# Store issue, layer norm steps and weight splitting rearranged in a kernel of spectral and sliding-window layers

## The chip, the cores and the metric

The kernel runs on one core of one Trainium2 chip. The time is the device time of one execution in microseconds (us); three executions of the kernel before gave 2269.78, 2270.76 and 2272.49 us, median 2270.76 us. One profiled execution gives the trace from which everything below is read.

## The reference

Four layers work on x of 2048 rows (S) and 640 columns (D), all in float32: a spectral (FNet) layer, a sliding-window attention block, and both again with the same weights. Each adds to x a function of the layer norm of x.

```python
# spectral: real part of a DFT over the columns, then over the rows
a = einsum("bsd,ed->bse", x, dft_hid_re);  b = einsum("bsd,ed->bse", x, dft_hid_im)
y = einsum("ts,bse->bte", dft_seq_re, a) - einsum("ts,bse->bte", dft_seq_im, b)
# attention: 32 heads of 20, each row sees itself and the 255 rows before it
q, k, v = split(x @ wqkv);  p = softmax(mask(q k^T * 20**-0.5));  out = (p v) @ wo
# layer norm, without weights: (x - mean) / sqrt(var + 1e-5)
```

## The kernel before, in words

Every float32 operand of TensorE is kept as two float16 parts, hi and lo; a product of two operands takes three float16 matmuls (hi·hi, hi·lo, lo·hi) that add up in PSUM. In almost every split ScalarE writes hi (an ACTIVATE that casts), and VectorE or GpSimd writes lo (the value less hi).

**The spectral layer.** x is 16 tiles of 128 rows. For each tile a `z_stage` makes the DFT over the columns (tiles `zc`). Then come four passes r over groups of 4 tiles of x, and in each pass eight steps j, each for two output tiles. A step (r, j) multiplies with seven combinations of blocks of the row DFT matrix, so that 7 products stand in place of 8: 7 products of 12 matmuls (128 columns by 320). The matrix blocks come as one 1 MB load `cq` per step (`load_c`, L170 through the helper `load`), two steps ahead. `take_c` makes the seven combinations of the next step: GpSimd forms four sums `cs` (L473 to L476), ScalarE writes each hi part `cc` (L481) and VectorE each lo part (L484). The products leave PSUM by one ACTIVATE (L520) and six VectorE adds (L507) per step, and GpSimd adds three more pieces (L521, L531, L542). The sums gather in two `res` tiles per step; there are 4 buffers. In passes 1 to 3 `res` is first loaded from `acc_d`; at the end of a step (`main_c`, L556) it is stored to `acc_d`, in the last pass to `x2_d`.

**What runs beside it.** `tick()` is called after each product (7 times a step). It issues one waiting split of `cc` and moves each generator of the list `side` to its next `yield`. So the number of `yield`s in a generator sets how it is spread over the products. In the first spectral layer the side generators are: `side_norm` (layer norm of one tile of x for the next pass, 12 in all, at j = 3, 4, 6, 7), `keep_w` (stores of the split column DFT matrix), `b_max` (largest values of the attention weights, 20 reductions), then `b_scale` and `b_split`, which scales, splits and stores the attention weights in 15 chunks of 128 by 640: ScalarE writes scaled hi (L653), VectorE scaled lo (L655, tile `bst`), ScalarE's queue stores both (L658). In pass 3 of both spectral layers `finish` normalizes the first tiles of the result for the attention (two tiles at a time), and `ahead` makes the first q and k products (`qk`) from them. `fill_stack` loads the first `ks` tiles of the attention at j = 7.

**Layer norm.** `norm_steps` takes n = 1 or 2 tiles at once: mean and variance on VectorE (L127, L130), then the inverse root in a column of n values: four TENSOR_SCALARs (L134 to L137: add epsilon, a shift and a subtraction on the bits for a first guess, a scaled copy), then three Newton steps (L141 and L145 for n = 1; L143, L144 and L145 for n = 2), tile `lnt`. The last step, (x − mean)·g over 128 by 640, is VectorE's L149, tile `lny`. `split` then writes `xs` (ScalarE L161, GpSimd L162). There are 30 calls with n = 1 and 17 with n = 2: 2 and 1 at the start, 12 in `side_norm`, 4 (n = 2) in `finish`, and 16 and 12 in the attention blocks. That makes 64 tiles.

**What sets the order.** Each engine runs its instructions in the order in which they were issued to its queue, and a DMA issue that has to wait holds up what is behind it on the engine that issues it. All loads go through `load`, on SyncE (SP). The 160 stores of this change (128 of `res`, 30 of `bst`, 2 of the column DFT matrix) are on ScalarE's queue; the stores of the q and k products (`qkd`) are on SP already.

Of the kernel before, what the change touches and what calls it, by code (L numbers as in the profile page):

```python
# [13 lines left out]
I32 = mybir.dt.int32  # L14
# [31 lines left out]
BACK_LAG = 15  # L46
M_UP = 2.0 ** 15
# [4 lines left out]
X_UP = 2.0 ** 10  # L52
# [8 lines left out]
def body(ctx: ExitStack, tc: tile.TileContext, x_in, cmat, whid, wqkv, wo, out):  # L61
# [58 lines left out]
    def norm_steps(xs, ys):  # L120

        n = len(xs)
        mv = keep.tile([P, n, 2], F32, tag=f"lnmv{n}", name="lnmv", bufs=2)
        for k, x in enumerate(xs):
            st = keep.tile([P, 2, 6], F32, tag="lnst", name="lnst", bufs=2)
            for h in range(2):
                nc.vector.bn_stats(st[:, h], x[:, h * 320:(h + 1) * 320])  # L127
                if h == 0:
                    yield
            nc.vector.bn_aggr(mv[:, k], st.rearrange("p a b -> p (a b)"))  # L130
            yield
        t = keep.tile([P, 3, n], F32, tag=f"lnt{n}", name="lnt", bufs=2)
        v, g, u = t[:, 0], t[:, 1], t[:, 2]
        nc.vector.tensor_scalar(v, mv[:, :, 1], 1e-5, X_UP ** -2, op0=OP.add, op1=OP.mult)  # L134
        nc.vector.tensor_scalar(g.bitcast(I32), v.bitcast(I32), 1, None, op0=OP.logical_shift_right)
        nc.vector.tensor_scalar(v, v, -0.5, None, op0=OP.mult)
        nc.vector.tensor_scalar(g.bitcast(I32), g.bitcast(I32), -1, 0x5F3759DF, op0=OP.mult, op1=OP.add)  # L137
        yield
        for k in range(3):
            if n == 1:  # L140
                nc.vector.scalar_tensor_tensor(u, g, v, g, op0=OP.mult, op1=OP.mult)  # L141
            else:
                nc.vector.tensor_tensor(u, g, g, op=OP.mult)  # L143
                nc.vector.tensor_tensor(u, u, v, op=OP.mult)  # L144
            nc.vector.scalar_tensor_tensor(g, u, 1.5, g, op0=OP.add, op1=OP.mult)  # L145
            yield
        for k, x in enumerate(xs):
            y = keep.tile([P, D], F32, tag="lny", name="lny", bufs=2)
            normed[0] = nc.vector.tensor_scalar(y, x, mv[:, k, 0:1], g[:, k:k + 1],  # L149
                                                op0=OP.subtract, op1=OP.mult).ins  # L150
            ys.append(y)
            yield
# [187 lines left out]
    def spectral(layer, res_src, hidden, first):  # L340
        with ExitStack() as st:
# [95 lines left out]
            def side_norm(s):  # L437
                x, ys = load_x(s), []
                for _ in range(3):
                    yield 1  # L440
                for _ in norm_steps([x], ys):
                    yield 1
                split_x(s, ys[0], nc.gpsimd)
                yield 1
# [101 lines left out]
            def main_c(r, j):  # L546
# [8 lines left out]
                for k in range(2):  # L555
                    nc.scalar.dma_start((x2_d if last else acc_d)[2 * j + k], res[k])  # L556
# [16 lines left out]
            def finish(j, pace):  # L573
# [6 lines left out]
                for _ in norm_steps(xs, ys):  # L580
                    for _ in range(pace):
                        yield 1
                for y in ys:
                    xs = keep.tile([P, 2, D], F16, tag="xs", name="xs", bufs=2)
                    split(xs[:, 0], xs[:, 1], y, nc.gpsimd)
                    xss.append(xs)
                    yield 1
# [18 lines left out]
            def b_max():  # L606
# [3 lines left out]
                for n in range(20):  # L610
# [3 lines left out]
                    for _ in range(2):  # L614
                        yield 1
# [29 lines left out]
            def b_split(n0, n1):  # L645
# [3 lines left out]
                for n in range(n0, n1):  # L649
# [3 lines left out]
                    nc.scalar.activation(hi, f, AF.Copy, scale=sc)  # L653
                    yield 1
                    nc.vector.scalar_tensor_tensor(lo, f, sc, hi, op0=OP.mult, op1=OP.subtract)  # L655
                    cs = slice((n % 3) * D, (n % 3 + 1) * D)
                    for k in range(2):
                        nc.scalar.dma_start(bw_d[k][:, n // 3, cs], t[:, k])  # L658
# [5 lines left out]
            def keep_w():  # L664
                for k in range(2):
                    nc.scalar.dma_start(w_d[k], w[:, k].rearrange("p a b c -> p (a b c)"))
# [20 lines left out]
            for r in range(NR):  # L687
# [22 lines left out]
                for j in range(NJ):  # L710
                    n = r * NJ + j
                    if first:
                        if (r, j) == (0, 1):
                            side.append(chain(keep_w(), b_max()))
                        if (r, j) == (1, 0):
# [584 lines left out]
```

## Time and profile before

| | |
|---|---|
| runs | 2269.78, 2270.76, 2272.49 us |
| the profiled execution | 2268.34 us, its span 2266.6 us |
| granted TensorE clock, mean of the span | 0.988 |
| PE (TensorE) busy | 2131.3 us, 94% |
| DVE (VectorE) busy | 1699.9 us, 75% |
| POOL (GpSimd) busy | 1364.0 us, 60% |
| ACT (ScalarE) busy | 1263.9 us, 56% |

Times in the trace are counted from the span's start. The first spectral layer takes about the first 600 us, the first attention block the next 550, the second spectral layer ends near 1700 us, the second attention block is the rest. A row of windows gives, for a stretch, its length and for PE, weight loads (PEld), DVE, ACT and POOL the busy us and, in brackets, the number of instructions; then the granted clock, the share of the DMA engines that was busy, and GB/s. A row of groups has line, engine, operation, out<-in, shape, count | busy us, mean ns of one | idle us of the engine just before them and what ended it. A row of waits has who waited <- for whom: us in all, times, longest. A row of the timeline has start, duration, engine, line, operation.

### The profile page before, as it was taken

To read this page: it belongs to the slowest core of one execution; us is meant where nothing else is said; L and a number is where in the kernel's file an instruction comes from. 1 tells how busy PE (TensorE), PEld (TensorE's weight loads), DVE (VectorE), ACT (ScalarE), POOL (GpSimd) and SP (SyncE) were. 2 spreads that over 40 slices of the span, in tenths; PEclk is the share of its full clock that TensorE was granted. 3 is DMA by queue.
4 is the path that set the end of the run, shared out by engine and by line. 5 is a ranking of instruction groups with operands and counts; after the bars stand their busy time and mean duration, and the time that the engine had idled before them with its cause. 6 is when DMAs were issued, how large, how long until landed. Compare 5 with 4: busy or idle time off the path is not lost.

```text
span 2266.6 us, 55134 instructions
## 1 busy us (share of the span) xinstructions
PE 2131.3 (94%) x21985; PEld 1498.0 (66%) x21985; DVE 1699.9 (75%) x3601; ACT 1263.9 (56%) x2120; POOL 1364.0 (60%) x1773
## 2 busy tenths in 40 slices
PE   7989899999899999999899999999898999999997
PEld 5667567667566676667556777777675666667765
DVE  7887969867678888887757858585776877777664
ACT  5334344343367777777754343434334777777775
POOL 5766758757355655566445858586683555556543
PEclk9999999999999999999999999999999999999999
DMA  5763656454432422332324536354643323332231
GB/s 190 281 223 124 230 161 208 145 198 163 134 77 69 107 70 69 95 90 75 133 73 149 197 122 207 119 201 146 236 140 97 83 61 86 79 90 68 55 81 36
DMA packets 187606, 292.95 MB, mean 129 GB/s; under 512 B 13908, under 2 KB 120660, under 8 KB 178004
## 3 DMA queue, kind: packets, MB, share of 16 engines
q1 hardware_dynamic: 163732, 238.63, 35.2%
q10 hardware_dynamic: 23616, 50.80, 6.1%
q8 instruction: 172, 2.82, 0.5%
q14 instruction: 86, 0.70, 0.1%
HBM read 202.51 MB, written 86.87 MB: 128 GB/s over the span
## 4 chain that ended last, share of the span: by engine, by line
PE 66%; DVE 21%; DMA 5%; issue 4%; ACT 2%; POOL 2%; SPq 0%; DVEq 0%; ACTq 0%; POOLq 0%
PE pf L114 26%; PE y L114 9%; PE pv L114 8%; PE z L114 6%; PE x L114 6%; PE sp L114 5%; DVE cc L484 5%; DVE m L1054 3%; PE tp L114 3%; DVE sp L1050 2%; PE pt L114 2%; DVE res L507 1%; DVE lnt L145 1%; DMA x2d<-res 1%; DVE lny L149 1%
## 5 line engine op out<-in xcount | busy, mean ns | idle before, releaser
L114 PEld LDWEIGHTS <-cc 128*128 128x128 f16 x5376 | 529.3, 99 | 245.8 <-issue 38.3
L1098 ACT ACTIVATE ptq<-tp,shift,alpha 128x768 f32<-128x768 f32 (+2 forms) x512 | 486.2, 950 | 161.7 <-PE tp L114 153.2
L114 PEld LDWEIGHTS <-big 128*128 128x128 f16 x4320 | 407.7, 98 | 136.4 <-issue 26.1
L1054 DVE TENSOR_REDUCE m<-sp 128x2 f32<-128x512 f32 (+1 forms) x512 | 345.1, 674 | 17.2
L1050 DVE COPY_PREDICATED sp<-mask,sp 128x256 f32<-128x256 int32 x448 | 190.6, 426 | 183.6 <-PE sp L114 168.3
L1103 POOL TENSOR_SCALAR_AFFINE_SELECT ptq<-ptq 128x512 f32<-128x512 f32 x224 | 145.9, 651 | 278.7 <-ACT ptq L1098 273.2
L114 PE MATMUL pf<-early,big 128*128 128x256 f16 x2400 | 313.3, 273 | 0.0
L481 ACT ACTIVATE cc<-cs 128x512 f16<-128x512 f32 x256 | 152.3, 623 | 249.4 <-POOL cs L474 100.6
L114 PE MATMUL y<-zc,cc 128*128 128x320 f16 x1728 | 270.9, 305 | 14.5 <-DVE pf L507 14.5
L114 PE MATMUL pf<-big 128*128 128x320 f16 x1680 | 242.2, 301 | 9.1 <-DVE early L252 4.2
L484 DVE SCALAR_TENSOR_TENSOR cc<-cs,cc 128x512 f16<-128x512 f32 x256 | 232.6, 924 | 3.6 <-ACT cc L481 3.6
L484 DVE SCALAR_TENSOR_TENSOR cc<-cq,cc 128x512 f16<-128x512 f32 x192 | 201.8, 1052 | 0.0
L1105 POOL TENSOR_SCALAR_AFFINE_SELECT ptq<-ptq 128x512 f32<-128x512 f32 x256 | 163.1, 637 | 42.5 <-ACT ptq L1098 42.5
L114 PE MATMUL z<-zc,cc 128*128 128x320 f16 x1152 | 179.7, 301 | 6.3 <-DVE res L507 6.3
L114 PE MATMUL pv<-ptq,v 128*32 128x128 f32 (+1 forms) x3840 | 183.8, 331 | 0.0
L114 PE MATMUL x<-zc,cc 128*128 128x320 f16 x1152 | 181.6, 301 | 0.0
L114 PE MATMUL sp<-ks,qs 62*128 62x256 f16 (+1 forms) x1792 | 153.3, 248 | 23.7 <-DVE m L1054 20.2
L114 PE MATMUL pf<-big,early 128*128 128x320 f16 x960 | 163.0, 300 | 8.1 <-DVE x L875 8.1
L114 PE MATMUL tp<-qs,ks 62*128 62x128 f16 x2688 | 150.1, 217 | 4.3 <-ACT ptq L1098 3.8
L1075 ACT ACTIVATE qs<-pt 2x512 f16<-2x512 f16 x224 | 130.9, 585 | 38.3 <-PE pt L114 36.3
L114 PE MATMUL pf<-bo,ot 128*128 128x320 f16 x840 | 144.1, 300 | 1.6 <-DVE ot L948 1.6
L114 PEld LDWEIGHTS <-ks 62*128 62x128 f16 x3008 | 116.1, 94 | 42.7 <-DVE m L1054 20.0
(144 smaller groups left out, 3526.8 us busy)
## 6 DMA issues: line engine op xcount, KB each, us to landing
cq<-in_cmat_dram SPq DMA_DIRECT2D x64, 1024.0 KB
accd<-res ACTq DMA_DIRECT2D x96, 320.0 KB
res<-accd SPq DMA_DIRECT2D x96, 320.0 KB
x<-x2d SPq DMA_DIRECT2D x64, 320.0 KB
qkd<-early SPq DMA_DIRECT2D x160, 128.0 KB
ks<-qkd SPq DMA_DIRECT2D x108, 160.0 KB
qs<-qkd SPq DMA_DIRECT2D x84, 160.0 KB
x2d<-res ACTq DMA_DIRECT2D x32, 320.0 KB
```

The source lines that it names most:

```text
L114: i = getattr(nc.tensor, what)(*args, **kw)
L145: nc.vector.scalar_tensor_tensor(g, u, 1.5, g, op0=OP.add, op1=OP.mult)
L149: normed[0] = nc.vector.tensor_scalar(y, x, mv[:, k, 0:1], g[:, k:k + 1], op0=OP.subtract, op1=OP.mult).ins
L481: nc.scalar.activation(cc[m][:, 0], f, AF.Copy, scale=C_UP)
L484: nc.vector.scalar_tensor_tensor(cc[m][:, 1], f, C_UP, cc[m][:, 0], op0=OP.mult, op1=OP.subtract)
L507: marks["dve"] = nc.vector.scalar_tensor_tensor(o, z, Y_DOWN, f, op0=OP.mult, op1=OP.add).ins
L1050: nc.vector.copy_predicated(sp[:, :, 2 * P:3 * P], mask[:, None, :].to_broadcast([P, 2, P]), far)
L1054: topped[0] = nc.vector.tensor_reduce(TOP[g // 4][:, g % 4], sp[:, :, c0:3 * P], axis=AX.X, op=OP.max).ins
L1075: nc.scalar.activation(o, handed[n][rs].rearrange("r (i p) t -> r i p t", i=2), AF.Copy)
L1098: nc.scalar.activation(q[:, h:h + 2, a0 + first:a0 + 3], tp[:, :, first * P:3 * P].rearrange("p a (b c) -> p a b c", c=P), AF.Sigmoid, bia ...
L1103: nc.gpsimd.affine_select(out=q[:, :, a0], in_=q[:, :, a0], pattern=[[0, 4], [-1, P]], base=0, channel_multiplier=1, compare_op=OP.is_gt, ...
L1105: ins = nc.gpsimd.affine_select(out=q[:, :, a0 + 2], in_=q[:, :, a0 + 2], pattern=[[0, 4], [1, P]], base=0, channel_multiplier=-1, compare ...
```

## The change

Four things:

1. The stores of `res`, of `bst` and of the column DFT matrix go through `load`, so on SP's queue, in order with the loads.
2. `norm_steps` works on one 128x1 column per tile. Every step is a TENSOR_SCALAR with one tensor input and up to two per-partition scalars; the first guess is one step (a multiplication by −0.5 and an addition on the bits as integers). A call with n = 1 has 8 such steps instead of 10, one with n = 2 has 16 instead of 13. `side_norm` and `finish` call it with `act=True`: then one more step per tile makes −mean·g, the last step over 128 by 640 is ScalarE's `activation(Identity, bias, scale)`, and two more `yield`s stand ahead of it. That moves 20 of the 64 `lny` from VectorE to ScalarE. All root steps together go from 521 to 532.
3. `b_split`: ScalarE scales the chunk in place and writes hi (two ACTIVATEs), GpSimd subtracts (L663), in place of one ACTIVATE and VectorE's L655.
4. Pacing: `b_scale` and `b_split` start at step (1, 2) instead of (1, 0); `b_max` has one more `yield` per chunk; `finish` has three more beside those of the norm, so that `qk` comes later.

Lines above L141 shift by up to 8: L170 is L175 in the changed kernel, L484 is L489, L507 is L512, L473 to L476 are L478 to L481.

```diff
-        v, g, u = t[:, 0], t[:, 1], t[:, 2]
-        nc.vector.tensor_scalar(v, mv[:, :, 1], 1e-5, X_UP ** -2, op0=OP.add, op1=OP.mult)
-        nc.vector.tensor_scalar(g.bitcast(I32), v.bitcast(I32), 1, None, op0=OP.logical_shift_right)
-        nc.vector.tensor_scalar(v, v, -0.5, None, op0=OP.mult)
-        nc.vector.tensor_scalar(g.bitcast(I32), g.bitcast(I32), -1, 0x5F3759DF, op0=OP.mult, op1=OP.add)
-        yield
-        for k in range(3):
-            if n == 1:
-                nc.vector.scalar_tensor_tensor(u, g, v, g, op0=OP.mult, op1=OP.mult)
-            else:
-                nc.vector.tensor_tensor(u, g, g, op=OP.mult)
-                nc.vector.tensor_tensor(u, u, v, op=OP.mult)
-            nc.vector.scalar_tensor_tensor(g, u, 1.5, g, op0=OP.add, op1=OP.mult)
+        ts = nc.vector.tensor_scalar
+        for k in range(n):
+            h, g, u = (t[:, m, k:k + 1] for m in range(3))
+            ts(h, mv[:, k, 1:2], 1e-5, -0.5 * X_UP ** -2, op0=OP.add, op1=OP.mult)
+            ts(g.bitcast(I32), h.bitcast(I32), -0.5, ROOT, op0=OP.mult, op1=OP.add)
+            for m in range(3):
+                ts(u, g, g, h, op0=OP.mult, op1=OP.mult)
+                normed[0] = ts(g, u, 1.5, g, op0=OP.add, op1=OP.mult).ins
+                if m == 0:
+                    yield
+            if act:
+                normed[0] = ts(u, mv[:, k, 0:1], g, -1.0, op0=OP.mult, op1=OP.mult).ins
+            yield
+        for _ in range(2 if act else 0):
             yield
         for k, x in enumerate(xs):
+            g, u = t[:, 1, k:k + 1], t[:, 2, k:k + 1]
             y = keep.tile([P, D], F32, tag="lny", name="lny", bufs=2)
-            normed[0] = nc.vector.tensor_scalar(y, x, mv[:, k, 0:1], g[:, k:k + 1],
-                                                op0=OP.subtract, op1=OP.mult).ins
+            if act:
+                nc.scalar.activation(y, x, AF.Identity, bias=u, scale=g)
+            else:
+                normed[0] = ts(y, x, mv[:, k, 0:1], g, op0=OP.subtract, op1=OP.mult).ins
...
                 for k in range(2):
-                    nc.scalar.dma_start((x2_d if last else acc_d)[2 * j + k], res[k])
+                    load((x2_d if last else acc_d)[2 * j + k], res[k])
...
+                    yield 1
+                for _ in range(2):
                     yield 1
                 proj.new_rows(j)
...
-                    nc.scalar.activation(hi, f, AF.Copy, scale=sc)
+                    nc.scalar.activation(f, f, AF.Copy, scale=sc)
+                    nc.scalar.activation(hi, f, AF.Copy)
                     yield 1
-                    nc.vector.scalar_tensor_tensor(lo, f, sc, hi, op0=OP.mult, op1=OP.subtract)
+                    nc.gpsimd.tensor_tensor(lo, f, hi, op=OP.subtract)
                     cs = slice((n % 3) * D, (n % 3 + 1) * D)
                     for k in range(2):
-                        nc.scalar.dma_start(bw_d[k][:, n // 3, cs], t[:, k])
+                        load(bw_d[k][:, n // 3, cs], t[:, k])
...
-                        if (r, j) == (1, 0):
+                        if (r, j) == (1, 2):
                             side.append(chain(b_scale(), b_split(0, 15)))
```

On VectorE, inside pass 1 or 2 of the first spectral layer, a side norm stands between the lo parts (`cc`) and the adds (`res`, `pf`). Before, with a chunk of `b_split` (`bst`) just ahead of it:

```order
L655 SCALAR_TENSOR_TENSOR bst<-wst,wsc,bst 128x640
L134 TENSOR_SCALAR lnt<-lnmv 128x1
L507 SCALAR_TENSOR_TENSOR res<-y,res 128x320
L135 TENSOR_SCALAR lnt<-lnt 128x1
L484 SCALAR_TENSOR_TENSOR cc<-cq,cc 128x512
L136 TENSOR_SCALAR lnt<-lnt 128x1
L137 TENSOR_SCALAR lnt<-lnt 128x1
L141 SCALAR_TENSOR_TENSOR lnt<-lnt 128x1
L145 SCALAR_TENSOR_TENSOR lnt<-lnt 128x1
L507 SCALAR_TENSOR_TENSOR pf<-y,pf 128x320
```

The same kind of place in the changed kernel, where line 140 and 141 are the two steps of a Newton round and L145 makes −mean·g:

```order
L489 SCALAR_TENSOR_TENSOR cc<-cs,cc 128x512
L137 TENSOR_SCALAR lnt<-lnmv 128x1
L138 TENSOR_SCALAR lnt<-lnt 128x1
L140 TENSOR_SCALAR lnt<-lnt 128x1
L141 TENSOR_SCALAR lnt<-lnt 128x1
L512 SCALAR_TENSOR_TENSOR pf<-y,pf 128x320
L489 SCALAR_TENSOR_TENSOR cc<-cs,cc 128x512
L140 TENSOR_SCALAR lnt<-lnt 128x1
L489 SCALAR_TENSOR_TENSOR cc<-cs,cc 128x512
L141 TENSOR_SCALAR lnt<-lnt 128x1
```

The two-input steps on `lnt` and the chunk of `bst` are gone from VectorE's queue; the lo parts and adds stay.

On GpSimd, in pass 1 of the first spectral layer, one step j of sums `cs` and adds to `res`. Before, with the split of a normed tile (`xs`) in it:

```order
L521 TENSOR_TENSOR res<-res,pf 128x320
L473 TENSOR_TENSOR cs<-cq 128x512
L475 TENSOR_TENSOR cs<-cq 128x512
L474 TENSOR_TENSOR cs<-cs,cq 128x512
L476 TENSOR_TENSOR cs<-cq,cs 128x512
L531 TENSOR_TENSOR res<-res,pf 128x320
```

Now:

```order
L526 TENSOR_TENSOR res<-res,pf 128x320
L478 TENSOR_TENSOR cs<-cq 128x512
L480 TENSOR_TENSOR cs<-cq 128x512
L479 TENSOR_TENSOR cs<-cs,cq 128x512
L663 TENSOR_TENSOR bst<-wst,bst 128x640
L481 TENSOR_TENSOR cs<-cq,cs 128x512
L536 TENSOR_TENSOR res<-res,pf 128x320
```

A chunk of the weights stands ahead of the fourth sum.

On SP, in the first spectral layer (the numbers tell the tiles apart: accd6 is the seventh tile of `acc_d`, `cq` the matrix blocks of a step, `wst` and `xin` chunks of the weights and of x). Before, only loads:

```order
L170 DMA res_2757<-accd6_117 128x640
L170 DMA res_2758<-accd7_118 128x640
L170 DMA cq_2748<-in_cmat_dram 128x2048
L170 DMA wst_2837<-in_wqkv_dram 128x640
L170 DMA res_2910<-accd8_119 128x640
L170 DMA res_2911<-accd9_120 128x640
```

Now the stores of `res` and `bst` stand between them, the loads of accd8 and accd9 and of `cq` behind the stores of accd4 and accd5:

```order
L175 DMA accd4_115<-res_2580 128x640
L175 DMA bwd0_145<-bst_2795 128x640
L175 DMA accd5_116<-res_2581 128x640
L175 DMA bwd1_146<-bst_2795 128x640
L175 DMA res_2895<-accd8_119 128x640
L175 DMA xin_2918<-in_x_dram 128x640
L175 DMA res_2896<-accd9_120 128x640
L175 DMA cq_2886<-in_cmat_dram 128x2048
```

More of the change, by code (lines that the diff above doesn't have):

```diff
@@ L46 @@
 BACK_LAG = 15
+ROOT = float(0x5F3759DF - (1 << 22) - (1 << 30))
 M_UP = 2.0 ** 15
@@ L118, in body, with norm_steps @@
     matmul, transpose = partial(tensor, "matmul"), partial(tensor, "transpose")
-    def norm_steps(xs, ys):
+    def norm_steps(xs, ys, act=False):
         n = len(xs)
@@ L440, in side_norm @@
                     yield 1
-                for _ in norm_steps([x], ys):
+                for _ in norm_steps([x], ys, True):
                     yield 1
@@ L579, in finish @@
                 ys, xss = [], []
-                for _ in norm_steps(xs, ys):
+                for _ in norm_steps(xs, ys, True):
                     for _ in range(pace):
@@ L613, in b_max @@
                         fs.append(b_chunk(n + 3))
-                    for _ in range(2):
+                    for _ in range(3):
                         yield 1
@@ L665, in keep_w @@
                 for k in range(2):
-                    nc.scalar.dma_start(w_d[k], w[:, k].rearrange("p a b c -> p (a b c)"))
+                    load(w_d[k], w[:, k].rearrange("p a b c -> p (a b c)"))
                     yield 1
```

## The prediction

> **What bounds the kernel now.** I read the page's chain first. TensorE carries two thirds of it, VectorE a fifth, and ScalarE, GpSimd and SP almost none:
>
> ```profile
> PE 66%; DVE 21%; DMA 5%; issue 4%; ACT 2%; POOL 2%; SPq 0%; DVEq 0%; ACTq 0%; POOLq 0%
> ```
>
> Then the windows. The two spectral layers do the same products, but only the first has side norms and weight splits beside them. So I set 500 us of the first beside 500 us of the second, then the 200 us in which the weights are split, then 50 us of the second layer:
>
> ```profile
> 100.00:600.00 500.00, 461.89 (x3391) 329.40 (x3389) 392.96 (x708) 196.39 (x383) 329.70 (x276) 0.97 0.55 183
> 1200.00:1700.00 500.00, 491.13 (x3642) 354.91 (x3641) 355.67 (x562) 197.02 (x398) 355.98 (x299) 0.99 0.51 170
> 250.00:450.00 200.00, 183.65 (x1329) 129.74 (x1329) 167.82 (x293) 86.31 (x164) 137.32 (x109) 0.97 0.55 183
> ...
> 1500.00:1550.00 50.00, 49.88 (x369) 35.81 (x367) 41.42 (x57) 19.46 (x37) 42.44 (x31) 1.00 0.61 207
> ```
>
> PE is idle 38.1 us in the first stretch and 8.9 in the second: 29.2 us more. The clock costs another 461.89 x 0.02/0.99 = 9.3. So the first layer runs 38 us behind the second. DVE is busy 393 us of the 500 there against 356. The longest waits of PE in the first stretch name DVE:
>
> ```profile
> PE y L114 <- DVE pf L507: 19.7, 9, 4.2
> PE pf L114 <- DVE early L252: 4.2, 2, 3.2
> ```
>
> L507 is the add that frees a PSUM bank; it comes late because other work stands ahead of it on DVE. The lower clock belongs to the stalls, as PE's timeline shows just behind one: these 12 matmuls take 3.15 us, the same 12 take 1.79 in the row after.
>
> ```profile
> 252.99 3.15 PE L114 MATMUL y<-zc,cc 128*128 128x320 f16 x12 [4.18 <-DVE pf L507]
> 255.98 1.79 PE L114 MATMUL x<-zc,cc 128*128 128x320 f16 x12
> ```
>
> **Root steps and lny.** Three windows of 100 to 600 us, each of one tile, give what the change touches on DVE: `lnt` (steps and lny together), `lny`, `bst`.
>
> ```profile
> 100.00:600.00 500.00, 62.71 (x162) 0.97 0.55 183
> ```
>
> ```profile
> 100.00:600.00 500.00, 16.48 (x16) 11.70 (x16) 25.30 (x16) 0.97 0.55 183
> ```
>
> ```profile
> 100.00:600.00 500.00, 20.82 (x15) 12.28 (x15) 0.97 0.55 183
> ```
>
> The steps alone are 62.7 - 16.5 = 46.2 us for 162 - 16 = 146 instructions (12 norms of n = 1 by 10, 2 of n = 2 by 13). The change makes them 12 x 9 + 2 x 18 = 144. Nothing is won by their number, so all hangs on the duration of one. The same window's groups, and the whole trace's figures for L141 (min/median/max):
>
> ```profile
> L141 DVE SCALAR_TENSOR_TENSOR lnt<-lnt 128x1 f32<-128x1 f32 x36 | 14.1, 391 | 0.5
> ...
> L135 DVE TENSOR_SCALAR lnt<-lnt 128x1 int32<-128x1 int32 x12 | 1.8, 148 | 0.2
> ```
>
> ```profile
> L141 DVE SCALAR_TENSOR_TENSOR lnt<-lnt x90: 203/214/1230, 6.8 to 1205.5; 128x1 f32<-128x1 f32 x90
> ```
>
> Two tensor inputs took 391 ns in the mean but 214 in the median; one input took 148. The timeline shows where the long ones come from:
>
> ```profile
> 382.34 1.60 POOL L476 TENSOR_TENSOR cs<-cq,cs 128x512 f32<-128x512 f32 x1
> ...
> 382.91 0.15 DVE L135 TENSOR_SCALAR lnt<-lnt 128x1 int32<-128x1 int32 x1
> ...
> 383.91 1.30 POOL L531 TENSOR_TENSOR res<-res,pf 128x320 f32<-128x320 f32 x1
> 384.42 0.81 DVE L141 SCALAR_TENSOR_TENSOR lnt<-lnt 128x1 f32<-128x1 f32 x1
> ```
>
> L141 ends about when GpSimd's L531 does, at 385.2; L135 ran its 0.15 us inside GpSimd's L476. So a two-input step waits for GpSimd and a one-input step does not. The new steps have one tensor input, but two per-partition scalars, which no step of the trace has in a 128x1 column. Bounds: 148 ns (one input) gives 144 x 0.148 = 21.3 us, a saving of 24.9; 391 ns (two inputs, with waits) gives 56.3, a loss of 10.1. I take L141's undisturbed 214, since the scalars have to be read: 30.8 us, saving 15.4. The rule that speaks against it stands in the Trainium skill, VectorE: DVE Perf Modes, "Rules for kernel authors": for chained operations, do not fuse for speed, minimize their number. By that rule 146 against 144 saves nothing; the rows of 148 and 391 ns at equal size say that number alone does not decide here.
>
> All 16 lny of the window leave DVE: 16.5 us. ScalarE takes them, at
>
> ```profile
> L161 ACT ACTIVATE xs<-lny 128x640 f16<-128x640 f32 x16 | 11.7, 731 | 23.5 <-DVE lny L149 23.5
> ```
>
> 0.73 us each for the same size: 12 us, and 15 more ACTIVATEs in b_split another 12, on an engine busy 196 of 500. Its cover is that idle time; if ACT's high parts came late by it, the price is in the next paragraph's halves.
>
> **b_split.** DVE loses all 15 L655: 20.8 us. GpSimd gains 15 subtractions of 128x640, priced by its nearest row of this window:
>
> ```profile
> L162 POOL TENSOR_TENSOR xs<-lny,xs 128x640 f16<-128x640 f32 x16 | 25.3, 1581 | 12.4 <-ACT xs L161 12.4
> ```
>
> 15 x 1.58 = 23.7 us. While they run, DVE's two-input lo parts can wait: from 0 to all of 23.7; I take half, 11.9. DVE thus goes down by 15.4 + 16.5 + 20.8 - 11.9 = 40.8, to 352 of 500, and GpSimd up to 353: the levels of the second layer (356 and 356), where PE loses 38 us less.
>
> I do not take all of it. The chunks come every 6 ticks; 6 products of 1.79 us are 10.7, so all 15 fall within 161 us, inside the 250:450 stretch. GpSimd there goes to (137.3 + 23.7)/200 = 80%. Excess of that stretch: 16.35 idle + 183.65 x 0.02/0.99 = 3.7, less 8.87 x 0.4 = 3.5 as in the second layer: 16.5. I take half back, 8, and of the other 22 all but 3, since b_max's reductions stay on DVE: 19. Together **27 us**, bounds 0 to 38.
>
> **Stores on SP.** 160 issues leave ACT. The waits of ACT in the window and of SP in the whole trace:
>
> ```profile
> ACT cc L481 <- DVE res L507: 20.0, 11, 3.9
> ```
>
> ```profile
> SPq L170 <- DMA accd<-res: 316.9, 84, 12.5
> ...
> SPq L170 <- DVE bst L655: 49.9, 12, 17.7
> ```
>
> ACT's high part stood behind a store that waited for `res`: 20 us go, off the path (ACT has room; 2% of the chain). SP already waits for these very stores to land before it reloads the same four buffers, 3.8 us on the mean, and for `bst`, up to 17.7 us; `cq` comes two steps ahead. So I price the move at nothing; the cover is that step in hand, and the price without it is a rival.
>
> **Layer ends and attention.** At the end of the second spectral layer (1640 to 1730 us) PE waits for DVE's adds:
>
> ```profile
> PE z L114 <- DVE res L507: 2.3, 1, 2.3
> ...
> PE y L114 <- DVE pf L507: 0.6, 1, 0.6
> PE sp L114 <- DVE res L507: 0.6, 1, 0.6
> ```
>
> 3.5 us per layer. In each layer's `finish` 4 lny leave DVE and 26 steps become 36 shorter ones. I take 2 of the 3.5 back per layer: **4 us**. Bounds: 8 and -5, the latter if the `qk` products, 4 products (7 us) later by their yields, leave the first attention rows late by 2.5 us per layer.
>
> In the attention blocks lny stays; `lnt` and then `lny` in the two blocks:
>
> ```profile
> 600.00:1200.00 600.00, 82.90 (x257) 0.98 0.32 87
> 1720.00:2266.00 546.00, 36.26 (x90) 1.00 0.28 70
> ```
>
> ```profile
> 600.00:1200.00 600.00, 22.23 (x27) 19.86 (x27) 36.40 (x26) 0.98 0.32 87
> 1720.00:2266.00 546.00, 12.31 (x12) 8.84 (x12) 16.77 (x12) 1.00 0.28 70
> ```
>
> The steps are 60.7 + 24.0 = 84.6 us in 308 instructions. They become 16 x 8 + 12 x 16 = 320, at 0.214 us 68.5: 16.1 us less. By DVE's share of the chain, 21%, that is worth **3 us**; bounds 0 and 8 (half).
>
> **Sum.** 27 + 4 + 3 = 34 off the profiled execution's 2268.3 gives 2234.3. The median of the runs, 2270.8, is 2.4 above that execution; so 2236.7, **2237 us**, 34 (1.5%) under. About 0.2% (4.5 us) is what a measurement of this kernel tells from no change.
>
> **Rivals.**
>
> *All comes back* (0.10). The first layer becomes as fast as the second: 38 + 8 + 8 = 54 off, 2217. For it: in 1500:1550 GpSimd is busy 42.44 of 50 and PE loses 0.1. Against it: that layer has no chunks between the sums.
>
> *GpSimd becomes the bound while the weights are split* (0.20). A chunk ahead of a sum or an add delays it by 1.58 us, and lo parts and PSUM banks behind it. Then the 16.5 us stay and a third of 23.7 comes on top: 19 - 8 + 4 = 15 off, 2253 + 2.4 = 2256. For it: the order puts L663 between L479 and L481. The Trainium skill's GPSIMD Engine Reference, "Key points", says that VectorE is about twice as fast at elementwise work. By that rule the chunks would take 15 x 2 x 1.39 = 42 us instead of 23.7, an estimate; the 1.58 beside DVE's 1.39 for one shape does not bear it out.
>
> *The steps are no cheaper* (0.09). With two scalars read from SBUF they wait like two-input steps: 521 instructions become 532 at the old mean. DVE then wins 16.5 + 20.8 - 11.9 = 25.4 of 40.8: 27 x 0.62 = 17, and 2 at the ends: 19 off, 2252. It is the rule on numbers above as a mechanism. If this and the one before come together (0.04), 11 - 8 + 2 = 5 are left: 2266, at the edge of no change.
>
> *SP stands in front* (0.09), on the other side. A store that waits for `res` or `bst` now stops the loads of `res` and `cq` behind it. This row of GpSimd in the first window shows that `res` is already late at times, 15.3 us in 29 adds:
>
> ```profile
> L531 POOL TENSOR_TENSOR res<-res,pf 128x320 f32<-128x320 f32 x29 | 35.2, 1215 | 31.1 <-DVE pf L507 15.8 <-DMA res<-accd 15.3
> ```
>
> If a third of SP's 3.8 us, 1.25, came through to PE in each of the 48 steps that reload `res`, 60 us would be lost, 26 more than won: 2268.3 + 26 + 2.4 = 2297. It decides against the change from 0.7 us per step (34/48). Against it: the reload already waited for that store's landing, whoever issued it.
>
> **How the numbers follow.** Forecast 0.48, rivals 0.10, 0.20, 0.09, 0.04, 0.09. Faster by over 0.2% are all but the last two: 0.87; within 0.2%: 0.04; slower: 0.09. The forecast's own range is 2217 to 2256, from its bounds; the range that takes in both middle rivals with a few us around them is 2216 to 2262.
>
> **What would show it.** Right: in 100:600 DVE near 352, GpSimd near 353, PE idle near 17 us, the waits "y <- DVE pf" well under 19.7; steps of `lnt` near 214 ns; no L655 on DVE. Wrong: steps at 390 ns; L663 on GpSimd with cs or res late behind it; SP's waits for `res` in the chain, or PE waiting for `cc` or `res<-accd`. If PE idles as much as before although DVE is down by 40, DVE's load was not the cause.

## The result and the profile after

The changed kernel takes 2234.28 us (median of 4 runs, 2231.40 to 2238.80) against 2270.27 us (4 runs, 2264.66 to 2272.49): a ratio of 0.9847, 95% interval 0.9823 to 0.9871, or 36 us less. The forecast was 2237, range 2216 to 2262. The total came out as forecast; its three terms did not, and their errors cancel, which is luck. The rest of this document is about that.

(Two slips in the section on the change: `finish` has two added `yield`s beside the two of the norm, not three, and the prediction's four products are right. The GpSimd rows shown there for the kernel before hold no `xs`.)

The profiled execution of the changed kernel took 2234.67 us, span 2233.0. The chain of the page reads

```profile
PE 59%; DVE 12%; DMA 4%; issue 3%; POOL 2%; ACT 2%; SPq 1%; DVEq 0%; POOLq 0%; ACTq 0%
```

DVE's 12% must not be set beside the 21% of before. These shares add up to 83%: followed back from the end, this chain reaches only to 391.9 us, so it leaves out passes 0 and 1 and part of pass 2, where the other one has much of its DVE. Over the same stretch, from that place on, DVE has 16% of the chain before and 14% now.

The windows that the prediction used, of the changed kernel:

```profile
100.00:600.00 500.00, 466.36 (x3446) 333.19 (x3445) 370.13 (x685) 220.46 (x416) 354.06 (x303) 0.98 0.56 184
...
250.00:450.00 200.00, 181.86 (x1315) 128.57 (x1313) 147.72 (x252) 95.38 (x179) 156.53 (x122) 0.96 0.54 181
```

GpSimd's 354 is the forecast's 353, and DVE went down by 23 to 370 (forecast 352). But PE's idle time in 100 to 600 us fell only from 38.1 to 33.6 us (forecast near 17), and in 250 to 450 us PE did less than before, 181.9 us against 183.7, though DVE had 20 us less to do. Here are PE's waits in 100 to 600 us:

```profile
PE pf L115 <- DVE zc L257: 9.3, 4, 5.3
PE pf L115 <- DVE early L257: 9.3, 2, 7.3
PE pf L115 <- POOL xs L167: 4.3, 2, 2.5
PE y L115 <- DVE pf L512: 3.5, 6, 1.0
```

The wait for the adds that free a bank, 19.7 us before, is 3.5. In its place stand waits for the z stages (`zc`, `early`, 3.1 and 4.2 before) and for the transposes of normed tiles (`xs`). So a fixed window does not say where the 34 us of the two profiles went. For that I take the same instruction in both programs, the first add of a step, `res<-x`, and compare when it runs. Before, at step (3, 0) and (3, 7) of the first spectral layer, and at (0, 0), (3, 0) and (3, 7) of the second:

```profile
480.87 0.49 DVE L507 SCALAR_TENSOR_TENSOR res<-x,res 128x320 f32<-128x320 f32 x1
599.37 0.49 DVE L507 SCALAR_TENSOR_TENSOR res<-x,res 128x320 f32<-128x320 f32 x1 [5.21 <-DMA res<-accd]
1225.42 0.48 DVE L507 SCALAR_TENSOR_TENSOR res<-x,res 128x320 f32<-128x320 f32 x1
1596.67 0.49 DVE L507 SCALAR_TENSOR_TENSOR res<-x,res 128x320 f32<-128x320 f32 x1 [0.47 <-PE x L114]
1713.16 0.49 DVE L507 SCALAR_TENSOR_TENSOR res<-x,res 128x320 f32<-128x320 f32 x1 [4.87 <-DMA res<-accd]
```

The same five in the changed kernel:

```profile
475.81 0.49 DVE L512 SCALAR_TENSOR_TENSOR res<-x,res 128x320 f32<-128x320 f32 x1
587.45 0.49 DVE L512 SCALAR_TENSOR_TENSOR res<-x,res 128x320 f32<-128x320 f32 x1 [2.76 <-DMA res<-accd]
1203.16 0.48 DVE L512 SCALAR_TENSOR_TENSOR res<-x,res 128x320 f32<-128x320 f32 x1
1573.50 0.49 DVE L512 SCALAR_TENSOR_TENSOR res<-x,res 128x320 f32<-128x320 f32 x1 [0.47 <-PE x L115]
1681.94 0.49 DVE L512 SCALAR_TENSOR_TENSOR res<-x,res 128x320 f32<-128x320 f32 x1 [2.45 <-DMA res<-accd]
```

The lead is 5.1 us after passes 0 to 2 of the first layer, 11.9 before the attention block, 22.3 behind it, 23.2 at the second layer's last pass and 31.2 at its end. So passes 0 to 2, where I had put 27 us, gave 5; the two last passes, where I had put 4, gave 7 and 8; the first attention block, where I had put most of 3, gave 10. The table shows the same stages for the kernels below, each against the profile of before, in us. Passes 0 to 2 are parted at step (1, 0) (200.51 us before); the last column is the span.

```
                             first layer           attn 1  second layer    attn 2   span
                             p0    p1-2   p3               p0-2   p3
changed                     -7.1   +2.1   -6.9   -10.3     -0.9   -8.0     -2.4   -33.6
stores on SP alone          -2.9   -0.6   -2.0    -0.0     -0.0   -0.2     -0.8    -6.6
short steps alone           -3.4   -3.9   -3.5   -10.4     -0.9   +0.2     +0.2   -21.7
changed, split on DVE       -7.1   -4.2   -6.8   -12.0     -1.0   -8.8     -0.9   -40.7
changed, lny on DVE         -7.5   -0.3   -9.3   -13.8     -0.6   -8.2     -2.9   -42.5
changed, both on DVE        -5.1   -0.1   -9.1   -12.9     -0.9   -8.3     -2.8   -39.2
changed, stores on ACT      -2.3   +1.8   -6.4    -6.9     -0.9   -4.9     -1.7   -21.4
changed, finish early       -5.1   +2.1   -4.5   -13.5     -0.9   -3.5     -0.5   -26.1
changed, weights early      -7.2   -0.9   -9.1   -12.6     -0.9   -6.3     -0.4   -37.4
steps with two inputs       +1.7   -2.4   -1.1    +3.2     -0.6   +0.7     +6.4    +7.9
the least change            -5.2   -1.9   -7.5   -13.3     -0.9   -8.5     -1.2   -38.5
changed, start at (1, 3)    -8.1   +2.2   -5.4   -12.9     -0.9   -7.5     -3.3   -35.9
changed, once more          -7.0   +2.5   -6.3   -12.0     -0.9   -5.8     -1.6   -31.1
```

The first and the last row are two profiles of the same kernel: they differ by up to 2.2 us in a stage. The row above the last, whose kernel differs from them in passes 1 and 2 alone, stands up to 2.6 us from them in other stages. So differences of one profile under about 3 us are not read. Two of the profiled executions were the slowest of their four: short steps alone (2246.57 us, 5.6 over the median) and stores on ACT (2246.93, 6.5 over), so these two rows show less than the medians gained.

The kernels were measured in several batches; the kernel before had medians of 2269.4 to 2270.7 us in them, so medians are compared across batches. The changed kernel has eight runs in two batches, 2230.35 to 2238.80 us, with a mean of 2234.2. The 6 to 7 us by which kernels with one part undone stand away from it are three to five times the standard error of that difference of means.

### The profile page after: what moved, and what is told of

It is laid out like the page before. It is cut to its first block, busy times and chain, and to the rows that moved or that the text cites. A ratio compares the mean times of both kernels' runs of the same rounds, so it can differ in the third digit from the quotient of the medians.

```text
span 2233.0 us, 55112 instructions
## 1 busy us (share of the span) xinstructions
PE 2122.0 (95%) x21985; PEld 1494.7 (67%) x21985; DVE 1646.4 (74%) x3577; ACT 1288.8 (58%) x2155; POOL 1391.6 (62%) x1788
## 4 chain that ended last, share of the span: by engine, by line
PE 59%; DVE 12%; DMA 4%; issue 3%; POOL 2%; ACT 2%; SPq 1%; DVEq 0%; POOLq 0%; ACTq 0%
PE pf L115 24%; PE pv L115 8%; PE y L115 7%; PE sp L115 5%; PE x L115 5%; PE z L115 5%; PE tp L115 3%; DVE m L1062 3%; DVE sp L1058 2%; PE pt L115 2%; DVE cc L489 1%; DMA res<-accd 1%; DMA x2d<-res 1%; PE acc L115 1%; DMA qs<-qkd 1%
## 5 line engine op out<-in xcount | busy, mean ns | idle before, releaser
L115 PE MATMUL y<-zc,cc 128*128 128x320 f16 x1728 | 263.8, 300 | 2.4 <-DVE pf L512 2.4
L489 DVE SCALAR_TENSOR_TENSOR cc<-cs,cc 128x512 f16<-128x512 f32 x256 | 255.2, 1012 | 9.9 <-ACT cc L486 9.7
L489 DVE SCALAR_TENSOR_TENSOR cc<-cq,cc 128x512 f16<-128x512 f32 x192 | 198.7, 1036 | 0.0
L115 PE MATMUL pv<-ptq,v 128*32 128x128 f32 (+1 forms) x3840 | 183.7, 330 | 0.0
L115 PE MATMUL sp<-ks,qs 62*128 62x256 f16 (+1 forms) x1792 | 153.6, 248 | 20.8 <-DVE m L1062 18.6
L167 POOL TENSOR_TENSOR xs<-lny,xs 128x640 f16<-128x640 f32 x63 | 94.2, 1497 | 83.3 <-ACT xs L166 82.6
```

The source lines that it names most:

```text
L115: i = getattr(nc.tensor, what)(*args, **kw)
L167: eng.tensor_tensor(lo, y, hi, op=OP.subtract)
L489: nc.vector.scalar_tensor_tensor(cc[m][:, 1], f, C_UP, cc[m][:, 0], op0=OP.mult, op1=OP.subtract)
```

## The experiments

**Stores on SP alone.** The kernel before, with

```diff
-                    nc.scalar.dma_start((x2_d if last else acc_d)[2 * j + k], res[k])
+                    load((x2_d if last else acc_d)[2 * j + k], res[k])
```

and the same for `bst` and the column DFT matrix.

> The kernel before with one part of the change: the 160 stores of res, bst and the column DFT matrix go through the load helper, on SP. My theory (the stores are hidden on either queue, the gain is DVE's relief): 2270 us within 4, and ScalarE's waits in front of its high parts 20 us less. Rival (ScalarE standing behind stores was a cost at the layer ends, where the changed kernel won 15 us): 2255 to 2260, with passes 3 of both spectral layers 5 us shorter each. Other rival (SP in front of the loads): over 2280.

2262.25 us (10 runs; before 2269.90), ratio 0.9970, interval 0.9957 to 0.9983: 7.7 us less. My price of nothing was wrong, and the rival with SP in front of the loads too. Two of SP's waits there:

```profile
SPq L170 <- DVE res L507: 279.4, 99, 16.0
...
SPq L170 <- DMA accd<-res: 77.1, 78, 3.6
```

SP now waits 279 us for `res` to be complete, and only 77 in place of 317 for the stores to `acc_d` to land. With the stores to `x2_d` (19.9 us, 111.3 before) these waits are 376 us in all against 429, and most of them stand one step earlier in the same chain (result, store, reload). In 100 to 600 us ScalarE's waits for `res` in front of its high parts (20.0 us) are not among its waits any more, but its waits there for GpSimd's sums (`cs`) rose from 66.2 to 113.9 us; all its waits in front of high parts fell from 128 to 116. The gain is not where the first rival had it, 5 us in each last pass; the table spreads it over stages in amounts (2.9 us at most) that one profile does not tell from nothing.

**Short steps alone.** The kernel before with the new `norm_steps`, called without `act`.

> The kernel before with one part: the norms' root in one-input steps on 128x1 columns; lny stays on VectorE, the stores on ScalarE, b_split and the pacing as before. My theory (the first attention block won 10 us and the last 2 because its norms' steps no longer wait for GpSimd, and part of the gain in the layer ends is theirs): 2252, with the attention blocks 12 us shorter together. Rival (the attention blocks won by what reaches them from the layer ends, earlier qk stores and weights): under 4 us in the attention blocks, 2262 or more.

2240.97 us (4 runs), ratio 0.9882, interval 0.9855 to 0.9909: 29 us less, more than I expected, and four fifths of the whole change. The table has 10.4 us of it in the first attention block, as in the changed kernel: and the stores alone gave 0.0 there: that term is the steps'. The last pass of the second layer gained nothing. (Without `act`, a norm with n = 1 has two `yield`s in its steps in place of four, so here the pace changed too; the experiment with two inputs below keeps that pace.)

**Split on VectorE.** The changed kernel with

```diff
-                    nc.scalar.activation(f, f, AF.Copy, scale=sc)
-                    nc.scalar.activation(hi, f, AF.Copy)
+                    nc.scalar.activation(hi, f, AF.Copy, scale=sc)
                     yield 1
-                    nc.gpsimd.tensor_tensor(lo, f, hi, op=OP.subtract)
+                    nc.vector.scalar_tensor_tensor(lo, f, sc, hi, op0=OP.mult, op1=OP.subtract)
```

> The changed kernel with one part undone: b_split writes its lo part on VectorE again, with one ScalarE instruction in place of two (its stores stay on SP, its start at step (1, 2)). My theory (the 15 chunks on GpSimd cost passes 1 and 2 what the relief of VectorE won there; those passes lost 2.5 us against the kernel before): passes 1 and 2 win 6 us back, 2228. Rival (VectorE is the limit there, GpSimd has room): 20.8 us more on VectorE cost half of that, 2244.

2227.00 us (4 runs, 2224.05 to 2228.18): 7 us faster than the changed kernel, as the theory said, and the table has 6.3 of them in passes 1 and 2. The windows of 250 to 450 us say the same: with the chunks on VectorE the row is

```profile
250.00:450.00 200.00, 186.44 (x1359) 131.84 (x1357) 161.19 (x284) 90.44 (x172) 142.80 (x111) 0.97 0.55 183
```

VectorE is busy 13.5 us longer and GpSimd 13.7 us less than in the changed kernel, and PE does 4.6 us more. So VectorE had that room. That GpSimd had none does not follow: the experiment with the weights early leaves the chunks on GpSimd and is as fast. The groups of the changed kernel in 100 to 600 us show the chunk and the lo parts:

```profile
L663 POOL TENSOR_TENSOR bst<-wst,bst 128x640 f16<-128x640 f32 x15 | 24.1, 1609 | 2.6 <-ACT bst L661 2.6
```

```profile
L489 DVE SCALAR_TENSOR_TENSOR cc<-cs,cc 128x512 f16<-128x512 f32 x109 | 116.2, 1079 | 8.4 <-ACT cc L486 8.3
```

With the chunks on VectorE the same group reads

```profile
L489 DVE SCALAR_TENSOR_TENSOR cc<-cs,cc 128x512 f16<-128x512 f32 x109 | 105.8, 984 | 4.3 <-ACT cc L486 4.3
```

The same 109 lo parts took 10.4 us longer with the chunks on GpSimd. The other 81 (`cc<-cq`) took 2.0 less (88.4 against 90.4), so 8.4 us of the 20.8 that left VectorE came back in its lo parts. That the fourth sum came later, behind a chunk, is argued from the order; ScalarE's waits for it were near in both (8.8 and 7.3 us).

**The last norm step on VectorE.** The changed kernel with

```diff
-            if act:
-                normed[0] = ts(u, mv[:, k, 0:1], g, -1.0, op0=OP.mult, op1=OP.mult).ins
...
-            if act:
+            if False:
                 nc.scalar.activation(y, x, AF.Identity, bias=u, scale=g)
```

> The changed kernel with one part undone: the last step of the 20 norms in side_norm and finish is on VectorE again, without the step for -mean*g; the two added yields stay. My theory (a 128x640 step of VectorE in front of the adds was a main part of the stalls): 8 to 12 us slower, 2244, lost in passes 0 and 3. Rival (the short steps alone did it): 2234 within 3.

2228.28 us (4 runs, 2226.17 to 2230.59): 6 us faster. Both theories are wrong: the 16.5 us of `lny` that left VectorE were worth less than nothing. A wait came with the move, in 100 to 600 us of the changed kernel:

```profile
ACT lny L153 <- DVE lnt L145: 16.8, 10, 3.5
```

ScalarE stands at the last step until VectorE has made -mean*g, with the high parts and z copies behind it. But without the move ScalarE waits longer, at `xs`:

```profile
ACT xs L164 <- DVE lny L153: 29.2, 8, 6.1
```

and with the split on VectorE, a kernel 7 us faster than the changed one, the wait at the last step is 30.1 us. So this wait does not explain the 6 us. The table spreads them over passes 1 to 3 and the attention block, 2 to 4 us in each.

**Stores on ScalarE.** The changed kernel with the 160 stores as before.

> The changed kernel with one part undone: the 160 stores are on ScalarE's queue again. Alone, the stores on SP made the kernel before 7.6 us faster. Theory (ScalarE is freed of waits for res, whatever else is changed): 2241 us. Rival (with the short steps res is done earlier, so ScalarE waits little for it): 2234 within 3.

2240.45 us (4 runs), ratio 0.9870, interval 0.9844 to 0.9896: 6 us slower than the changed kernel, whose interval this one overlaps. So the stores are worth 6 to 8 us, with or without the rest.

**Both on VectorE.** The changed kernel with the split's lo part and the last norm step on VectorE.

> The changed kernel with two parts undone: b_split's lo part and the last norm step are on VectorE again; the short steps, the stores on SP and the pacing stay. Each undone alone gave 6 to 7 us. Theory (both moves cost by themselves, since the queues of GpSimd and ScalarE are stood in front of): they add up, 2221. Rival (VectorE has room for one of them only): 2227 or more.

2226.68 us (4 runs, 2223.99 to 2230.29). The two gains do not add up, as the rival had it; that VectorE has room for one of them only is not shown by that.

**Finish early.** The changed kernel with

```diff
-        for _ in range(2 if act else 0):
+        for _ in range(2 if act is True else 0):
...
-                for _ in norm_steps(xs, ys, True):
+                for _ in norm_steps(xs, ys, 2):
...
-                for _ in range(2):
-                    yield 1
                 proj.new_rows(j)
```

the first two in `norm_steps` and `finish`, so that `finish` alone loses its four yields.

> The changed kernel with the four added yields of finish taken out (two of the norm, two ahead of the transposes), so that the first q and k products come four products earlier. Theory (pass 3 of the second spectral layer won its 8 us by this pacing: neither the stores alone nor the steps alone shortened it): 8 us longer in that pass and some in the first layer's, 2242 to 2248. Rival (it won by the last norm step leaving VectorE; against that, the kernel with this step on VectorE kept the 8 us): 2234 within 3.

2240.07 us (4 runs), ratio 0.9862, interval 0.9838 to 0.9886: 6 us slower, though the intervals overlap. In the table the last pass of the second layer is 2.3 to 4.5 us longer than in the two profiles of the changed kernel. PE's waits there (1570 to 1695 us) begin with

```profile
PE pf L115 <- ACT early L401: 2.7, 1, 2.7
PE pf L115 <- POOL xs L167: 2.7, 2, 2.4
```

and in the changed kernel (1567 to 1690 us) with

```profile
PE y L115 <- DVE pf L512: 1.2, 2, 0.6
PE pf L115 <- POOL xs L167: 0.8, 1, 0.8
```

The transposes and q, k products of `finish` stand in PE's own queue. Issued four products earlier, they wait for their norm there, and the products behind them wait too: 2.7 and 2.7 us in these rows against 0.8. The kernel before had those waits (1.9 and 1.6 us, the rows `pf <- ACT early` and `pf <- POOL xs`).

**Weights early.** The changed kernel with `b_max` at 2 ticks and `b_scale` from step (1, 0).

> The changed kernel with b_max at 2 ticks per chunk and b_scale and b_split from step (1, 0), as before. Theory (pacing matters only for finish): 2234 within 3. Rival (pass 0 of the first layer won its 8 us by the slower reductions): 5 us longer in pass 0, 2239.

2227.69 us (4 runs, 2225.71 to 2230.97): 6 to 7 us faster. Neither theory had that. Pass 0 is unchanged (-7.2), so the slower reductions gave nothing there. This kernel has its chunks on GpSimd and its last norm steps on ScalarE, like the changed one, and in 250 to 450 us GpSimd is even busier, while PE does 6.3 us more than in the changed kernel:

```profile
250.00:450.00 200.00, 188.11 (x1350) 132.99 (x1351) 149.42 (x262) 96.21 (x181) 159.49 (x124) 0.95 0.53 180
```

So neither the two moves nor GpSimd's load cost the 6 us by themselves: in the kernels measured they are lost only where both moves and the later start, with its slower reductions, come together.

**Steps with two inputs.** The kernel with the short steps alone, with

```diff
-                ts(u, g, g, h, op0=OP.mult, op1=OP.mult)
-                normed[0] = ts(g, u, 1.5, g, op0=OP.add, op1=OP.mult).ins
+                nc.vector.scalar_tensor_tensor(u, g, h, g, op0=OP.mult, op1=OP.mult)
+                normed[0] = nc.vector.scalar_tensor_tensor(g, u, 1.5, g, op0=OP.add, op1=OP.mult).ins
```

> The kernel with the short steps alone (2241 us), with the same steps in number, place and size, but each of the six Newton steps with two tensor inputs in place of one tensor and per-partition scalars; the one-step first guess stays. Theory (a two-input step waits for GpSimd's operation on hand, a one-input step does not, and that is the gain of 29 us): steps over 350 ns in the mean with a maximum over 1 us, and most of the gain gone, 2262 within 5. Rival (the gain is in the shorter chain, 8 steps for 10, and in working tile by tile): 2241 within 4 with steps of any length.

2273.98 us (12 runs), ratio to the kernel before 1.0019, interval 1.0005 to 1.0033. All of the 29 us are gone, and 3 to 4 more. The work, the number of steps and their place in the code are the same; only the form differs (the order on the engines shifts a little with it). With two inputs, the Newton steps' figures over the whole trace are

```profile
L140 DVE SCALAR_TENSOR_TENSOR lnt<-lnt x192: 167/220/1223, 6.0 to 2086.9; 128x1 f32<-128x1 f32 x192
L141 DVE SCALAR_TENSOR_TENSOR lnt<-lnt x192: 142/160/1367, 6.2 to 2087.7; 128x1 f32<-128x1 f32 x192
```

and with one input

```profile
L140 DVE TENSOR_SCALAR lnt<-lnt x192: 220/272/275, 5.8 to 2056.6; 128x1 f32<-128x1 f32 x192
L141 DVE TENSOR_SCALAR lnt<-lnt x192: 195/214/216, 6.1 to 2056.9; 128x1 f32<-128x1 f32 x192
```

The one-input step has the longer median, 272 against 220 and 214 against 160 ns. But its longest is 275 ns, where the other's is 1367. Busy time of the 384 steps is 70.7 + 61.4 = 132 us with two inputs and 51.2 + 40.3 = 92 us with one.

What the long ones wait for can be counted in the two traces. With two inputs, 157 of the 384 steps took over 240 ns, and every one of the 157 ended 7 to 18 ns after an instruction of GpSimd ended. With one input, 229 of the 384 began while GpSimd was at work, and none took over 275 ns.

**The least, the same again, a shift.** The changed kernel with the split, the last norm step and the pacing of the weights as before; the changed kernel unaltered; and with `b_scale` from step (1, 3).

> The kernel before with what helped so far and no more: the short steps, the stores on SP, the added yields of finish and of the side norms; b_split and the last norm step on VectorE, b_max and b_split paced as before. Theory (each of the parts left out cost 6 to 7 us by itself): 2220 or less. Rival (they overlap, any one of them left out frees the same stretch): 2227 within 3, as the three kernels that leave out one.

> The changed kernel once more, unaltered, on the same chip as the two others of this job: 2234 within 3, so that the 6 to 7 us by which three kernels with one part undone were faster stand against it measured side by side.

> The changed kernel with b_scale and b_split from step (1, 3) in place of (1, 2), nothing else. Theory (the chunks on GpSimd cost time wherever they fall): 2234 within 3. Rival (what counts is which sums and adds a chunk happens to stand in front of, so that a shift of one step moves the time by as much as undoing a part): outside 2230 to 2238.

2227.55 us (5 runs), 2233.52 (4 runs) and 2234.58 (4 runs), on one chip. The repeat stands at 0.9835 (0.9815 to 0.9855) and the least change at 0.9804 (0.9785 to 0.9824). Their intervals overlap a little; the runs themselves, 2230.35 to 2237.21 and 2224.37 to 2229.79, do not. A shift by one step changes nothing. So the short steps, the stores on SP and the later `finish` give everything; moving the split and the last norm step to GpSimd and ScalarE, with the later start of the weights, takes 6 us back.

## Why the prediction was right in sum and wrong in its terms

**Right: the mechanism of the steps.** The forecast rested on a two-input step waiting for GpSimd and a one-input step not. The experiment with two inputs shows it: the gain of 29 us hangs on that form alone, and all the long steps end with an instruction of GpSimd. The price taken, 214 ns, was near in the mean: the changed kernel's `lnt` window of 100 to 600 us is

```profile
100.00:600.00 500.00, 29.24 (x139) 14.72 (x16) 0.98 0.56 184
```

where 139 steps took 29.24 us (210 ns) on VectorE; the forecast was 30.8 for 144. It was near by luck: 214 was the undisturbed step with two tensor inputs, and 210 is the mean of steps of about 145, 210 and 269 ns. The rule of the Trainium skill that I weighed there (VectorE: DVE Perf Modes, "Rules for kernel authors": do not fuse chained operations for speed, minimize their number) gave no gain from 146 steps against 144. The runs show the gain at equal number (192 + 192 in both kernels).

**Wrong in size: 27 us in the first layer.** Its passes 0 to 2 gave 5. The step that failed is the one from VectorE's relief to PE's time: "All 16 lny of the window leave DVE: 16.5 us" and "DVE loses all 15 L655: 20.8 us", and then "I take half back, 8, and of the other 22 all but 3". The prediction had named the sign: "If PE idles as much as before although DVE is down by 40, DVE's load was not the cause." DVE was down by 23, and PE idle 33.6 us where 38.1 had been and near 17 was forecast. PE's lost time did not go away, it moved from `pf` to `zc` and `early`; it does so with the short steps alone too (9.4 and 5.4 us there), so the two moves did not cause that. The least change settles what the relief was worth. It has `lny` and the chunks on VectorE, which is as busy in the window as in the kernel before (393.0):

```profile
100.00:600.00 500.00, 466.69 (x3455) 333.14 (x3453) 391.47 (x703) 199.18 (x388) 334.92 (x288) 0.98 0.56 185
```

and its passes 0 to 2 gain 7.1 us, the whole kernel 43. The kernel with the weights early differs from it by the two moves alone; its passes 0 to 2 gain 8.1, and it takes 2227.69 us against 2227.55. So on balance the 37.3 us of `lny` and `bst` were worth nothing. The short steps took 40 us less of VectorE than the same steps with two inputs, and the kernel 33 us less. Why the one kind of relief counts and the other does not was not settled, nor what holds PE in these passes: none of the kernels gains more than 11.2 us there.

The rival "GpSimd becomes the bound while the weights are split" had the right sign: in this kernel the move costs 6 to 7 us in passes 1 and 2 (split on VectorE), where the rival had the stretch's 16.5 and 8 more. As a mechanism it is not shown: with the weights early GpSimd is busy 159.5 of the same 200 us, more than the 156.5 of the changed kernel, and the 6 us are not lost. The half of 23.7 taken for waits of lo parts, 11.9, fits what was measured, 8.4 to 10.4. One reading of the trace was off: the chunks do not all lie in 250 to 450 us; four of the fifteen begin before 250 in the kernel before, two in the changed one.

**Wrong in cover: ScalarE.** "Its cover is that idle time" held on average (220 of 500 us busy) and failed in the end: the kernel without this move is 6 us faster. It fails only with the chunks on GpSimd and their later start beside it; with the weights early the move costs nothing.

**Wrong: the stores at nothing.** They are worth 6 to 8 us. I saw ScalarE's 20 us of waits for `res` and called them off the path by ScalarE's share of the chain, 2%. The share of an engine in one chain did not tell what its waits cost.

**Wrong in size: attention, 3 us.** It gave 10.3 and 2.4. The saving on VectorE was near the 16.1 forecast: between two equal marks of the first block (620 to 1134.5 us before, 607 to 1117.3 after) `lnt` fell from

```profile
620.00:1134.50 514.50, 73.63 (x222) 0.99 0.33 88
```

to

```profile
607.00:1117.30 510.30, 62.15 (x216) 0.00 (x0) 0.99 0.34 88
```

11.5 us, `lny` unchanged in both (20.4); in the second block the steps fell by 3.0, from 24.0 to 20.9. (The forecast's 16.1 sets 308 steps seen in its two windows against 320; the blocks had 316, and like for like it would have been about 18, an estimate.) Between these marks the block is 4.2 us shorter; 5.0 more came on the way from there to the second layer's first step. What failed is the conversion by 21%, VectorE's mean share of the chain: 14.5 us less on VectorE came with 12.7 us less time. An argument for it, not a proof: the share averages over stages, and in the attention block VectorE is busy 420 of 514 us.

**Wrong in size and in part in sign: layer ends, 4 us.** They gave 15. I counted the later `qk` as a possible loss of up to 5; finish early shows that the later issue is a gain of about 6, since PE no longer waits so long in its own queue for the norm.

Of the rivals, SP in front of the loads is refuted (stores alone: 7.7 us faster), and the steps being no cheaper too. 34 = 27 + 4 + 3 was forecast; the profile gave 5 + 15 + 13, and 1 more in passes 0 to 2 of the second layer.

**Open.** Why the chunks on GpSimd, the last norm step on ScalarE and the later start of the weights cost 6 to 7 us together was not settled. Leaving out one, two or all three of them gives 2227 to 2228 each time, so they take the same few microseconds, and none costs them alone. For the split the table has them in passes 1 and 2; for the others it spreads them over stages in amounts near the 2 to 3 us that two profiles differ by.

## What to carry to other kernels

Look at the minimum, median and maximum of a small operation, not only at its mean: here a form that did not wait won 29 us though its median is longer. When undoing either of two moves gives the same gain, undo their pacing too before one of them is blamed. When work is moved to an engine with room on average, read that engine in the stretch where the work falls, and who stands behind it in its queue. Price a term from its own stage, by marks that both programs pass, and not by a share of the whole chain: here the sum was right by luck, and each of its three terms was off by a factor of about four to five.

## What the runs showed of the hardware

A one-input step on a 128x1 column did not wait for GpSimd in 192 + 192 executions of the kernel with the short steps alone (longest 275 ns), 229 of which began during an instruction of GpSimd; the steps with one and two per-partition scalars are alike in this. Of the 175 two-input steps begun there in the experiment with two inputs, 147 took over 240 ns and ended just behind it (up to 1367 ns). On two columns one input was not enough in the kernel before. Its groups over the whole trace:

```profile
L135 DVE TENSOR_SCALAR lnt<-lnt 128x2 int32<-128x2 int32 x17 | 6.6, 391 | 0.6
...
L135 DVE TENSOR_SCALAR lnt<-lnt 128x1 int32<-128x1 int32 x30 | 4.5, 150 | 0.6
```

The same step took 391 ns in the mean on 128x2 and 150 on 128x1. That the 128x2 form waits shows in the single steps: of the 68 in L134 to L137 on 128x2, 21 took over 200 ns, and all 21 ended 22 to 28 ns after an instruction of GpSimd; of the 120 on 128x1 none took over 156. The Trainium skill, GPSIMD Engine Reference, "Key points", says that GpSimd shares its SBUF interfaces with VectorE and contends with VectorE's instructions that have two SBUF inputs or run in a 2-port mode; the trace agrees for two inputs (1367 ns at the longest), and no run here parts the modes. Working one column at a time, two sets of steps in place of one, took these waits away too; what that alone was worth no run measured. A second surprise: steps with per-partition scalars took longer, 269 ns with two (L140) and 211 with one (L141) against about 145 with constants alone (L137 and L138 of the changed kernel, 143 and 148 ns).
